# Turning the first-layer output of a fused attention and two-MoE kernel on the vector engine and the DMA queue

## The chip, the cores and the metric

The kernel runs on one core of one Trainium2 chip, in one launch. The metric is device time in microseconds. Three runs of the kernel before took 1084.47, 1084.37 and 1082.22 us, with a median of 1084.37. One execution was profiled: it took 1082.45 us, of which 1080.7 us lie between its first and its last instruction. Engines are named as in the profile: PE is the tensor engine's matmuls, PEld its weight loads, DVE the vector engine, ACT the scalar engine, POOL GpSimd, SP the engine that issues nearly all DMAs.

## The reference

Three layers follow each other, all in float32 except two weight matrices given as float64.

```python
# attention: 8 batches, 8 heads, 576 positions, head size 64, mask in blocks of 64
scores = q @ k.T / 8;  scores[block_i < block_j] = -1e9
attn = softmax(scores);  x = attn @ v                     # x: 4608 tokens x 512
# first dense pair (float64 weights): 512 -> 2048 -> 512
h = x @ w_in;  g = where(h > 0, h, exp(min(h, 0)) - 1);  y = g @ w_out
# soft mixture of 8 experts with 4 slots each
logits = y @ phi                                          # 4608 x 32
d = softmax(logits, over tokens);  slot_in = d.T @ y
slot_out[e] = relu(slot_in[e] @ w1[e]) @ w2[e]
out = softmax(logits, over slots) @ slot_out
```

## The kernel before

The kernel never forms y. It folds `phi` into `w_out` once (WP = w_out @ phi, 2048 x 32), takes the logits of a token straight from g, and gathers d.T @ g (32 slots x 2048) over all tokens; `w_out` is applied to that small result at the end.

The work is cut in four parts.

1. **Start.** 16 chunks each of `w_in` and `w_out` come in as raw float64 words, are narrowed on ACT or POOL and DVE, and become two rounded halves (w_in: `first_weights`) or a float32 copy in DRAM and WP (w_out: `second_weights`). Some space of later tiles serves as staging.
2. **Attention**, in 32 pairs of heads (`pair_load`, `pair_prep`, `pair_scores`, `pair_weights`, `pair_values`). Scores go through exp on ACT to an SBUF buffer PB (two copies, one per pair parity), are scaled on POOL, turned by 128x128 on PE (line 312, att), copied out and multiplied by V (lines 573 and 581). The product enters a ring of x columns, from which token tiles are read.
3. **Token tiles**, 36 of 128 tokens (`moe_tile`, the last two by `last_tiles`). A tile's x is split in two rounded halves (lines 598, 600). For each of four ranges r of 512 hidden units, `tile_range` runs 4 x 3 matmuls (lines 613 to 615) into one of two PSUM banks, ACT takes the exp (618), DVE finishes the nonlinearity (620, 623) into a slot of g. Then four 128x128 transposes on PE (line 312, g) turn the range into one PSUM bank, and ACT or DVE copies it (288 or 290) to gt. `tile_logits` multiplies gt with WP (line 636). After the four ranges `tile_dispatch` takes maxima and exps and adds d.T @ g (line 686) to an accumulator (690). A g slot is free again when line 686 has read it; there are six.
4. **Tail** (`tail`): 36 pieces of 1 MB each (w_out copy, w1, w2 of the experts) are loaded into space that becomes free (lines 749 and 763), the experts run (806, 827, 849), and the output is formed (916).

**What sets the order.** Nothing is left to a scheduler on the chip. `Plan.add` records each step with the engines that may do it, an assumed duration, what it reads and writes, and a key. `Plan.order` plays the steps through on the host, each free engine taking the ready step of the lowest key, and writes each engine's program in that order. So each engine runs a fixed list, and one that meets a wait holds all that stands behind it. SP's list holds the q, k and v loads, and at the end the 1 MB pieces. Where the played PE would be idle in the start or the tail, small bf16 filler matmuls are put in (line 948).

Of the kernel before, what the change touches and what calls it, by code (L numbers as in the profile page):

```python
# [18 lines left out]
P = 128  # L19
# [7 lines left out]
KWS, KWOS, KA0, KAS, KCON, KLD, KSTAGE, NPB = 3.5, 1.0, -109.0, 14.0, -98.0, 30.0, 26.0, 4  # L27
# [170 lines left out]
def attention_moe_kernel(ctx: ExitStack, tc, q, k, v, w_in, w_out, phi, w1, w2, consts, out):  # L198
# [34 lines left out]
    PB = aa.take(2 * PW)  # L233
    PAD = aa.take(12 * PIECE - aa.size)
# [86 lines left out]


    def start():
# [3 lines left out]
        def init(e):  # L327
            nc.vector.memset(f(ACC, 512), 0.0)
            nc.vector.memset(f(SM, 160), 0.0)
            nc.vector.memset(f(sum_col, 20), 1.0)  # L330
            nc.vector.memset(f(NMX, 2), 1e30)
# [3 lines left out]
        def zero(e):  # L335
            for s in range(2):
                nc.gpsimd.memset(f(PB + PW * s + S, 64), 0.0)
            for s in range(NV):
                nc.gpsimd.memset(f(V + 640 * s, 640, 64, P).rearrange("p (h x) -> p h x", h=2)[:, :, 256:320], 0.0)
        add("POOL", 0.9, zero, w=[("p", "b", s) for s in range(2)] + [("v", s, 2) for s in range(NV)], key=k0)  # L340


# [3 lines left out]
               [(GT + 1024 * j, 512, [("gt", 2 * j), ("gt", 2 * j + 1)]) for j in range(2)] + \  # L346
# [112 lines left out]
    def pair_scores(n, fill, key):  # L459
        s = n % 2  # L460
        qt, kt = QT + S * s, KT + S * s
        banks, bkeys = ((H0, H0 + 512), [("h", 0), ("h", 1)]) if n < 4 and fill % 2 else ((SB0, SB0 + 512), [("sb", 0), ("sb", 1)])
        units = FILLS[fill]

        def at(x):
            return banks[0] + 224 if x == "b" else banks[x[1]] + (384 if x[0] == 0 else 0)

        def keys(x):
            return bkeys if x == "b" else [bkeys[x[1]]]

        def sc(e):
            if fill == 0:
                for h, y in ((0, 0), (1, 1), (0, 1), (1, 0)):
                    mm(pb(at("b") + 288 * y, 288, 64 * h, 64 * h + 64), lhsT=f(qt + 512, 64, 64 * h, 64 * h + 64),  # L474
                       rhs=f(kt + 288 * y, 288, 64 * h, 64 * h + 64), start=True, stop=True)
                return
            for u, h in units:
                mm(pb(at((u, h)), P * (u + 1)), lhsT=f(qt + P * u, P, 64 * h, 64 * h + 64),  # L478
                   rhs=f(kt, P * (u + 1), 64 * h, 64 * h + 64), start=True, stop=True)
        cols = S if fill == 0 else sum(wide(x) for x in units) // 2  # L480
        add("PE", 0.2 + cols / 600, sc, r=[("qt", s), ("kt", s)], w=bkeys, key=key)
        for x in units:
            if x != "b":
                add("DVE", 0.11, lambda e, x=x: nc.vector.memset(pb(at(x) + P * x[0] + 64, 64, 0, 64), MASKED), w=keys(x), key=key)
        for x in units:
            c = nm_col + 9 * s + UNITS[x][0]
            add("DVE", 0.08 + wide(x) / 960, lambda e, x=x, c=c: nc.vector.tensor_reduce(  # L487
                out=f(c, 1), in_=pb(at(x), wide(x)), axis=AX.X, op=ALU.max, negate=True),
                r=keys(x), w=[("nm", s, x)], key=key)
            add("ACT", 0.42 + wide(x) / 1300, lambda e, x=x, c=c: nc.scalar.activation(  # L490
                f(PB + PW * s + UNITS[x][1], wide(x)), pb(at(x), wide(x)), AF.Exp, bias=f(c, 1), scale=1.0,
                accum_out=f(sum_col + 9 * s + UNITS[x][0], 1)),
                r=keys(x) + [("nm", s, x)], w=[("p", x, s), ("sum", s, fill // 2)], key=key)

    def pair_weights(n, half, key):
# [9 lines left out]
        for x in units:  # L505
            p = PB + PW * s + UNITS[x][1]
            add("POOL", 0.2 + wide(x) / 1050, lambda e, x=x, p=p: nc.gpsimd.tensor_scalar(  # L507
                out=f(p, wide(x)), in0=f(p, wide(x)), scalar1=f(rs_col + 9 * s + UNITS[x][0], 1), scalar2=0.0,
                op0=ALU.mult, op1=ALU.add), r=[("rs", s, half)], w=[("p", x, s)], key=key)
# [26 lines left out]
        for gi, (blocks, outs) in enumerate(groups):  # L536
            tb, tk = (POST, "post") if gi % 2 and n < NPB else (PTB, "ptb")

            def tr(e, blocks=blocks, tb=tb):
                for j, (x, c) in enumerate(blocks):  # L540
                    transpose(pb(tb + P * j, P), f(PB + PW * s + UNITS[x][1] + P * c, P))
            add("PE", 0.02 + 0.108 * len(blocks), tr, r=[("p", x, s) for x in {b[0]: 0 for b in blocks}] + ["con"], w=[tk], key=key, load=0.0)
# [20 lines left out]
    def pair_values(n, key):  # L563
# [7 lines left out]
        def first(e):  # L571
            for h in range(2):
                mm(pb(PTB, 64, 64 * h, 64 * h + 64), lhsT=f(vs + 320 * h, D), rhs=f(pts[h], 64), start=True, stop=True)
        add("PE", 0.17, first, r=rd, w=["ptb"], key=key, load=0.25)
        add(*evict(n, 64), lambda e: copy(e, f(XR + RING * p + ring, 64), pb(PTB, 64)), r=["ptb"], w=[("xr", p, b % 2, 0)], key=key)
        for c in range(5):
            q0 = max(64, P * c)

            def pv(e, c=c, q0=q0):
# [3 lines left out]
            add("PE", 0.02 + (S - q0) / 603, pv, r=rd, w=["pvb"], key=key, load=0.25)  # L583
# [5 lines left out]
    tslot = [(GT + 512 * j, ("gt", j)) for j in range(4)]  # L589
# [15 lines left out]
    def tile_range(i, r, hb, gs, ts, kr):  # L605
        s = i % 2
        xh, xl = XH + 512 * s, XL + 512 * s
        (g, gk), (gt, tk) = gs, ts
# [17 lines left out]

        def gtr(e):
# [3 lines left out]
        add(CP2, cpdur(512), lambda e: copy(e, f(gt, 512), pb(GTB, 512)), r=["gtb"], w=[tk], key=kr)  # L631

    def tile_logits(r, ts, bank, bk, kp):
# [4 lines left out]
        add("PE", 0.3, lg, r=["wp", ts[1]], w=[bk], key=kp, load=0.25)  # L638
# [55 lines left out]
    def moe_tile(i, key):  # L694
        gs = [gslot[(4 * i + r) % NG] for r in range(4)]
        tile_split(i, key - 6)
        for r in range(4):
            tile_range(i, r, r % 2, gs[r], tslot[r], key + 5.5 * r)
        for r in range(4):
            tile_logits(r, tslot[r], POST, "post", key + 17)  # L700
        tile_dispatch([i], [gs], [(POST, "post")], [(LPS, "lps")], (DTX, "dtx"), (DX, "dx"), key + 17)

    def last_tiles(i, key):

        order = [gslot[(4 * i + j) % NG] for j in range(NG)] + tslot[2:]
# [13 lines left out]
    def tail(key):  # L719
        att = [(nm, s, a) for nm in ("rq", "rk") for s in range(2) for a in range(4)] + [(nm, s) for nm in ("qt", "kt") for s in range(2)] + \  # L720
              [("v", s, j) for s in range(NV) for j in range(3)] + [("p", x, s) for x in UNITS for s in range(2)] + \
# [12 lines left out]
        slots = [(lambda j=j: f(PT + PIECE * j, PIECE).rearrange("p (c d) -> p c d", d=512), att) for j in range(12)]  # L734
        slots += [(ring(hf), xk[hf]) for hf in range(2)]
        slots += [(held("w%d" % r, j), wk[r]) for r in range(4) for j in range(2)]
        slots += [(held("xhl", 0), hk), (lambda: f(GT, PIECE).rearrange("p (c d) -> p c d", d=512), [("gt", r) for r in range(4)])]
# [118 lines left out]
        def late(x, n, dtype, p0=0, p1=P):  # L856
            nm = "w3" if x < 2 * PIECE else "xhl"
# [4 lines left out]
        for m in range(9):  # L862
            handover([("cpkh", m)], sum((pkeys(j) for j in ((20, 21) if m < 8 else (22,))), []))
        handover([("sop", 0), ("sop", 1)], pkeys(22))
# [38 lines left out]
        places = [p1[1, g][1] for g in range(4)] + [23]  # L903
# [79 lines left out]
```

## Time and profile before

| | before |
|---|---|
| median of three runs | 1084.37 us (1082.22 to 1084.47) |
| profiled execution | 1082.45 us, span 1080.7 us |
| PE busy | 1034.6 us, 96% of the span |
| DVE, ACT, POOL busy | 617.5, 499.5, 275.6 us |
| bytes moved by DMA | 97.95 MB, most in the first 150 us and the last 200 us |

A group of the profile reads: line, engine, operation, names written and read, shape, count, then busy us and the mean ns of one, then idle us of the engine just before and who ended most of it. A matmul in float32 stands as two records; a transposing one as one. The duration of a matmul contains its way through the array, so that the distance from one start to the next is what it costs on a full PE. `128*32` ahead of a shape says that the matmul uses a part of the array, 128 rows by 32 columns; four such run beside each other.

### The profile page before, as it was taken

What the parts mean: (1) busy time and instruction counts of PE and PEld (TensorE: products, weight loads), DVE (VectorE), ACT (ScalarE), POOL (GpSimd) and SP (SyncE); (2) the same over time, 40 slices, a digit from 0 to 9 for tenths busy, and PEclk for the clock granted to TensorE, in tenths of its full rate; (3) what the DMA queues carried; (4) which work ended last, traced back from release to release, by engine and by line L of the source; (5) the groups of instructions that cost most, each with busy time, mean ns of one, the idle gap of its engine ahead of it and who ended that gap; (6) DMA issues with size and microseconds to landing.
All of it is one profiled execution on the core that took longest, in us unless ns stands there. A gap on an engine that the chain in (4) does not pass through costs nothing.

```text
span 1080.7 us, 19505 instructions
## 1 busy us (share of the span) xinstructions
PE 1034.6 (96%) x7287; PEld 687.0 (64%) x7287; DVE 617.5 (57%) x1560; ACT 499.5 (46%) x1346; POOL 275.6 (26%) x396
## 2 busy tenths in 40 slices
PE   7878999999999999999999999999999999999993
PEld 4546676666666666666666666666766666767441
DVE  6989663455554555565756665656656564453241
ACT  3766453455454545454544534454444443332134
POOL 4886220122222313122323222231222222010000
PEclk9999889999999999999999999999999999999997
DMA  9988940011111111212111111121110024717969
GB/s 188 201 190 189 229 122 12 18 28 35 33 35 34 34 34 30 38 23 39 29 34 33 35 34 34 23 36 29 30 29 12 1 79 147 282 44 277 348 228 350
DMA packets 219486, 97.95 MB, mean 91 GB/s; under 512 B 192512, under 2 KB 192640, under 8 KB 219392
## 3 DMA queue, kind: packets, MB, share of 16 engines
q1 hardware_dynamic: 217616, 96.49, 34.4%
q8 instruction: 57, 0.93, 0.4%
q10 hardware_dynamic: 1776, 0.22, 0.2%
q14 instruction: 37, 0.30, 0.1%
HBM read 83.05 MB, written 13.63 MB: 89 GB/s over the span
## 4 chain that ended last, share of the span: by engine, by line
PE 86%; DMA 4%; DVE 3%; POOL 2%; SPq 1%; issue 1%; ACT 1%; ACTq 0%; DVEq 0%; POOLq 0%
PE ps L312 16%; PE ps L613 14%; PE ps L615 12%; PE ps L614 12%; PE ps L581 7%; PE ps L478 7%; PE ps L636 4%; PE ps L686 3%; PE ps L474 3%; PE ps L849 1%; POOL att L507 1%; PE ps L827 1%; SPq L307 1%; DMA wo_f<-att 1%; DVE att L374 1%; PE ps L652 1%
## 5 line engine op out<-in xcount | busy, mean ns | idle before, releaser
L613 PE MATMUL ps<-w,xhl 128*128 128x512 f32 x576 | 258.1, 448 | 0.0
L507 POOL TENSOR_SCALAR att<-att,base 128x128 f32<-128x128 f32 (+4 forms) x288 | 173.2, 619 | 246.8 <-DVE base L503 231.2
L615 PE MATMUL ps<-w,xhl 128*128 128x512 f32 x576 | 227.2, 394 | 0.4 <-POOL xhl L600 0.4
L614 PE MATMUL ps<-w,xhl 128*128 128x512 f32 x576 | 226.3, 393 | 0.0
L490 ACT ACTIVATE att<-ps,base 128x128 f32<-128x128 f32 (+4 forms) x288 | 157.4, 553 | 98.9 <-DVE base L487 94.6
L288 ACT COPY att<-ps 128x512 f32<-128x512 f32 (+3 forms) x217 | 106.1, 511 | 123.6 <-PE ps L312 119.0
L312 PE MATMUL ps<-base,att 128*128 128x128 f32 x864 | 140.9, 285 | 11.9 <-POOL att L507 7.4
L620 DVE TENSOR_SCALAR xe<-xe 128x512 f32<-128x512 f32 x144 | 67.6, 469 | 146.4 <-ACT xe L618 145.4
L487 DVE TENSOR_REDUCE base<-ps 128x1 f32<-128x128 f32 (+4 forms) x288 | 137.1, 506 | 23.4 <-PE ps L474 14.7
L312 PEld LDWEIGHTS ps<-base,att 128*128 128x128 f32 x864 | 102.4, 146 | 61.3 <-issue 22.7
L613 PEld LDWEIGHTS ps<-w,xhl 128*128 128x128 f32 x576 | 108.7, 189 | 48.9 <-issue 35.6
L618 ACT ACTIVATE xe<-ps 128x512 f32<-128x512 f32 x144 | 86.1, 598 | 88.5 <-PE ps L615 86.6
L615 PEld LDWEIGHTS ps<-w,xhl 128*128 128x128 f32 x576 | 108.2, 188 | 25.6 <-POOL xhl L600 0.9
L614 PEld LDWEIGHTS ps<-w,xhl 128*128 128x128 f32 x576 | 109.4, 190 | 10.1
L600 POOL TENSOR_TENSOR xhl<-xe,xhl 128x512 fp32r<-128x512 f32 x36 | 47.1, 1310 | 221.4 <-ACT xhl L598 187.7
L478 PE MATMUL ps<-att 64*128 64x128 f32 (+3 forms) x512 | 98.7, 478 | 4.8 <-ACT att L490 4.7
L623 DVE TENSOR_TENSOR g<-xe,ps 128x512 f32<-128x512 f32 x144 | 98.0, 680 | 3.3
L581 PE MATMUL ps<-att 128*64 128x512 f32 (+4 forms) x640 | 94.4, 427 | 0.0
L312 PE MATMUL ps<-base,g 128*128 128x128 f32 x592 | 90.3, 275 | 0.1
L288 ACT COPY g<-ps 128x512 f32<-128x512 f32 (+1 forms) x77 | 44.9, 584 | 87.0 <-PE ps L312 86.0
L312 PEld LDWEIGHTS ps<-base,g 128*128 128x128 f32 x592 | 70.1, 141 | 21.6 <-issue 4.9
L290 DVE COPY g<-ps 128x512 f32<-128x512 f32 (+1 forms) x77 | 52.5, 682 | 42.1 <-PE ps L312 41.5
(115 smaller groups left out, 1089.0 us busy)
## 6 DMA issues: line engine op xcount, KB each, us to landing
att<-in_moe_w_dram SPq DMA_DIRECT2D x12, 1024.0 KB, 13.7
att<-in_k_dram SPq DMA_DIRECT2D x127, 72.0 KB, 2.7
att<-in_q_dram SPq DMA_DIRECT2D x126, 72.0 KB, 2.6
att<-in_v_dram SPq DMA_DIRECT2D x64, 128.0 KB, 2.6
g<-in_moe_w_in_dram SPq DMA_DIRECT2D x16, 512.0 KB, 6.4
w_late<-in_moe_w_dram SPq DMA_DIRECT2D x8, 1024.0 KB, 6.6
att<-in_moe_w_dram SPq DMA_DIRECT2D x32, 256.0 KB, 5.8
out_dram<-att SPq DMA_DIRECT2D x16, 512.0 KB, 5.5
```

The lines of the kernel that those rows point to most:

```text
L288: nc.scalar.copy(o, i)
L312: mm(o, lhsT=i, rhs=f(IDN + base, n, base, base + n), start=True, stop=True, is_transpose=True)
L478: mm(pb(at((u, h)), P * (u + 1)), lhsT=f(qt + P * u, P, 64 * h, 64 * h + 64), rhs=f(kt, P * (u + 1), 64 * h, 64 * h + 64), start=True, sto ...
L487: add("DVE", 0.08 + wide(x) / 960, lambda e, x=x, c=c: nc.vector.tensor_reduce(out=f(c, 1), in_=pb(at(x), wide(x)), axis=AX.X, op=ALU.max, ...
L490: add("ACT", 0.42 + wide(x) / 1300, lambda e, x=x, c=c: nc.scalar.activation(f(PB + PW * s + UNITS[x][1], wide(x)), pb(at(x), wide(x)), AF ...
L507: add("POOL", 0.2 + wide(x) / 1050, lambda e, x=x, p=p: nc.gpsimd.tensor_scalar(out=f(p, wide(x)), in0=f(p, wide(x)), scalar1=f(rs_col + 9 ...
L581: mm(pb(PVB + q0 - 64, S - q0, 64 * h, 64 * h + 64), lhsT=f(vs + 320 * h + D * c, D), rhs=f(pts[h] + CHS * c + q0, S - q0), start=(c == 0) ...
L613: mm(pb(bank, 512), lhsT=fr(xh + P * kk, P), rhs=hi, start=(kk == 0), stop=False)
L614: mm(pb(bank, 512), lhsT=fr(xh + P * kk, P), rhs=lo, start=False, stop=False)
L615: mm(pb(bank, 512), lhsT=fr(xl + P * kk, P), rhs=hi, start=False, stop=(kk == 3))
L618: add("ACT", 0.48, lambda e: nc.scalar.activation(f(ee, 512), pb(bank, 512), AF.Exp), r=[("h", hb)], w=[("e", hb)], key=kr)
L623: add("DVE", 0.6, lambda e: nc.vector.tensor_tensor(out=f(g, 512), in0=f(ee, 512), in1=pb(bank, 512), op=ALU.max), r=[("e", hb), ("h", hb) ...
```

## The change

A tile's g is no longer turned on PE, except for the last two tiles. DVE turns 32x32 blocks within each 32 partitions and writes them, ordered by block, to a new buffer TT (two copies, one per tile parity). When all four ranges of the tile are there, 16 DMAs on SP carry block rows of 32 partitions to block columns of another 32 partitions of gt, 64 KB each. After that one run of 16 matmuls gives the logits.

```diff
-            add("PE", 0.44, gtr, r=[gk, "con"], w=["gtb"], ...)       # tiles 0 to 33
-            add(CP2, cpdur(512), ... copy(e, f(gt, 512), pb(GTB, 512)), r=["gtb"], w=[tk], ...)
+        if ts is None:
+            tt = f(TT + PIECE * s, PIECE).rearrange("p (b c j) -> p c b j", b=4, j=32)[:, 4 * r:4 * r + 4]
+            add("DVE", 0.7, lambda e: nc.vector.transpose(out=tt, in_=f(g, 512).rearrange("p (c b i) -> p c b i", c=4, i=32)),
+                r=[gk], w=[("tt", s, r)], key=kr)
+            return
...
+    def tile_turn(i, kp):
+        s = i % 2
+        for a in range(4):
+            for b in range(4):
+                load(f(GT + 512 * a, 512, 32 * b, 32 * b + 32), f(TT + PIECE * s + 512 * b, 512, 32 * a, 32 * a + 32), 1 << 16,
+                     r=[("tt", s, r) for r in range(4)], w=[("gt", a, b)], key=kp)
+        def lg(e):
+            gt = f(GT, PIECE).rearrange("p (a c j) -> p c a j", a=4, j=32)
+            for c in range(16):
+                j = c % 4
+                mm(pb(POST, P, 32 * j, 32 * j + 32), lhsT=f(WP + NS * c, NS), rhs=gt[:, c], start=(c < 4), stop=(c >= 12))
+        add("PE", 1.0, lg, r=["wp"] + sum((gtk(a) for a in range(4)), []), w=["post"], key=kp, load=0.25)
```

The five steps of a pair's values become one step, so that nothing of another kind stands among their matmuls. Space moves: six g slots become eight, PB has one copy instead of two, the attention area shrinks, and the bank of the g transposes serves half of the late pairs' transposes. The 1 MB pieces of the tail find nine places instead of twelve in the attention area, then the two of TT. The first pairs' keys are set wider apart.

```diff
-KWS, KWOS, KA0, KAS, ... = 3.5, 1.0, -109.0, 14.0, ...
+KWS, KWOS, KA0, KAS, ... = 3.5, 1.0, -116.0, 16.5, ...
-    NG = 6
+    NG = 8
+    TT = ga.take(2 * PIECE)
-    PB = aa.take(2 * PW)
+    PB = aa.take(PW)
-        add("PE", 0.17, first, ...); for c in range(5): add("PE", 0.02 + (S - q0) / 603, pv, ...)
+        add("PE", 2.9, pv, r=rd, w=["ptb", "pvb"], key=key, load=0.25)
-        slots = [(lambda j=j: f(PT + PIECE * j, PIECE)..., att) for j in range(12)]
+        slots = [(flat(PT + PIECE * j), att) for j in range(9)]
+        slots += [(flat(TT + PIECE * j), [("tt", j, r) for r in range(4)]) for j in range(2)]
```

PE in the middle of the program, before: a tile's logits in two runs (line 636), and its g transposes (line 312, g) among the first-layer matmuls and the transposes of attention (line 312, att).

```order
L636 MATMUL ps<-g,base 32x128 x12
L478 MATMUL ps<-att 128x384 x2
L478 MATMUL ps<-att 128x128 x2
L613 MATMUL ps<-w_68,xhl 128x512
L614 MATMUL ps<-w_68,xhl 128x512
L615 MATMUL ps<-w_68,xhl 128x512
L312 MATMUL ps<-base,att 128x128 x4
L312 MATMUL ps<-base,g 128x128 x4
L613 MATMUL ps<-w_68,xhl 128x512
L614 MATMUL ps<-w_68,xhl 128x512
L615 MATMUL ps<-w_68,xhl 128x512
L312 MATMUL ps<-base,att 128x128 x4
L636 MATMUL ps<-g,base 32x128 x4
```

PE in the middle of the changed program (the first-layer lines are 614 to 616 there, the logits line 652).

```order
L614 MATMUL ps<-w_70,xhl 128x512
L615 MATMUL ps<-w_70,xhl 128x512
L616 MATMUL ps<-w_70,xhl 128x512
L652 MATMUL ps<-g,base 32x128 x16
L614 MATMUL ps<-w_70,xhl 128x512
L615 MATMUL ps<-w_70,xhl 128x512
L616 MATMUL ps<-w_70,xhl 128x512
L674 MATMUL ps<-base 128x128
L675 MATMUL ps<-base 128x32
```

The g transposes are gone from the list, and a tile's logits stand in one run, which now waits for the last of the tile's 16 DMAs.

SP at the end of the attention, before: the last v loads, and then the 1 MB pieces, the w_out copy (wo_f) first.

```order
L307 DMA att<-in_v_dram 128x4x64 x2
L307 DMA att<-in_v_dram 64x2x64
L749 DMA att<-wo_f_73 128x4x512 x4
L749 DMA att<-in_moe_w_dram 128x2x1024 x8
L749 DMA xe<-in_moe_w_dram 128x4x512 x2
```

SP at the same place in the changed program. `g<-g` are the turning DMAs, 16 per tile; the names TT and gt lie in the area g.

```order
L308 DMA g<-g 32x512 x48
L773 DMA att<-wo_f_73 128x4x512 x4
L773 DMA att<-in_moe_w_dram 128x2x1024 x5
L773 DMA xe<-in_moe_w_dram 128x4x512
L308 DMA g<-g 32x512 x48
L773 DMA g<-in_moe_w_dram 128x2x1024
L773 DMA xe<-in_moe_w_dram 128x4x512
L308 DMA g<-g 32x512 x10
L773 DMA w_late_8387<-in_moe_w_dram 128x2x1024
L773 DMA w_late_8387<-in_moe_w_dram 128x4x512
L308 DMA g<-g 32x512 x6
```

Ten pieces of 1 MB now stand on SP between the turning DMAs of tile 29 and those of tile 30, and two more within those of tile 33.

## Rows read from the trace of the kernel before

**Rows 1.** The page: busy times of the engines, and shares of the last chain.
```profile
PE 1034.6 (96%) x7287; PEld 687.0 (64%) x7287; DVE 617.5 (57%) x1560; ACT 499.5 (46%) x1346; POOL 275.6 (26%) x396
...
PE 86%; DMA 4%; DVE 3%; POOL 2%; SPq 1%; issue 1%; ACT 1%; ACTq 0%; DVEq 0%; POOLq 0%
```

**Rows 2.** By stage: busy PE, PEld, DVE, ACT, POOL; clock, DMA share, GB/s.
```profile
0.00:91.00 91.00, 70.92 (x576) 46.91 (x576) 76.84 (x165) 53.80 (x144) 66.74 (x83) 0.94 0.94 191
...
150.00:930.00 780.00, 779.94 (x5369) 522.23 (x5368) 440.47 (x1182) 370.44 (x1029) 186.91 (x287) 1.00 0.18 41
...
995.00:1081.00 86.00, 65.40 (x551) 32.08 (x548) 26.50 (x52) 26.42 (x55) 0.00 (x0) 0.90 0.85 306
```

**Rows 3.** Groups by form: busy us, mean ns, idle before and its releasers.
```profile
L623 DVE TENSOR_TENSOR g<-xe,ps 128x512 f32<-128x512 f32 x144 | 98.0, 680 | 3.3
L312 PE MATMUL ps<-base,g 128*128 128x128 f32 x592 | 90.3, 275 | 0.1
L618 ACT ACTIVATE xe<-ps 128x512 f32<-128x512 f32 x144 | 86.1, 598 | 88.5 <-PE ps L615 86.6
...
L620 DVE TENSOR_SCALAR xe<-xe 128x512 f32<-128x512 f32 x144 | 67.6, 469 | 146.4 <-ACT xe L618 145.4
...
L290 DVE COPY g<-ps 128x512 f32<-128x512 f32 x76 | 52.1, 685 | 42.0 <-PE ps L312 41.5
...
L443 DVE STREAM_TRANSPOSE att<-att 128x576 f32<-128x576 f32 x64 | 48.4, 762 | 6.4 <-DMA att<-in_q_dram 4.3 <-DMA att<-in_k_dram 1.2 <-issue 0.8
```

**Rows 4.** PE in order of time: start us, us, line, shape, count.
```profile
403.36 0.60 PE L312 MATMUL ps<-base,g 128*128 128x128 f32 x4
403.72 0.48 PE L613 MATMUL ps<-w,xhl 128*128 128x512 f32 x1
404.03 0.40 PE L614 MATMUL ps<-w,xhl 128*128 128x512 f32 x1
404.27 0.40 PE L615 MATMUL ps<-w,xhl 128*128 128x512 f32 x1
...
410.32 0.40 PE L615 MATMUL ps<-w,xhl 128*128 128x512 f32 x1
410.65 0.64 PE L636 MATMUL ps<-g,base 128*32 128x128 f32 x16
```

**Rows 5.** DMA issue by line (ns, min/median/max), and times to landing at 142:149, 440:446, 42:62.
```profile
L763 SPq DMA_DIRECT2D att<-in_moe_w_dram x32: 327/362/2939, 1006.9 to 1039.5; - x32
...
L307 SPq DMA_DIRECT2D att<-in_q_dram x126: 328/490/2729, 0.7 to 782.9; - x126
...
wo_f<-att SPq DMA_DIRECT2D x3, 256.0 KB, 2.1
...
att<-in_q_dram SPq DMA_DIRECT2D x4, 72.0 KB, 2.5
...
att<-in_q_dram SPq DMA_DIRECT2D x7, 72.0 KB, 7.2
```

**Rows 6.** The 1 MB pieces: SP in order, landing at 906:922, the stage 920:930.
```profile
881.78 25.73 SPq L749 DMA_DIRECT2D att<-wo_f  x4
907.60 11.64 SPq L749 DMA_DIRECT2D att<-in_moe_w_dram  x8
...
att<-in_moe_w_dram SPq DMA_DIRECT2D x8, 1024.0 KB, 17.2
...
920.00:930.00 10.00, 10.00 (x66) 7.00 (x64) 4.88 (x11) 2.96 (x6) 0.37 (x1) 1.00 1.03 408
```

**Rows 7.** PE in a dispatch with nothing beside it, 998:1003.
```profile
998.81 0.49 PE L652 MATMUL ps<-base 128*128 128x128 f32 x2 [0.25 <-DVE base L648]
...
1001.08 0.44 PE L312 MATMUL ps<-base,xe 128*128 128x128 f32 x2 [0.30 <-ACT xe L661]
...
1002.11 1.48 PE L686 MATMUL ps<-g,xe 128*32 128x512 f32 x10 [0.32 <-DVE base L869]
```

**Rows 8.** The stage 140:150, columns as in rows 2.
```profile
140.00:150.00 10.00, 8.30 (x38) 6.94 (x39) 8.46 (x20) 6.45 (x20) 0.59 (x1) 0.65 0.42 150
```

More of the change, by code (lines that the diff above doesn't have):

```diff
@@ L320, in handover, with gtk @@
             plan.readers.setdefault(b, []).extend(sorted(ops))
+    def gtk(a):
+        return [("gt", a, b) for b in range(4)]
     def start():
@@ L411, in give_back @@
             handover(["c"], [("wot", 0), ("wot", 1)])
+            handover([("tt", 0, r) for r in range(4)], [("narrow", 0), ("narrow", 1)])
             handover([("e", 0), ("e", 1)] + [("xr", p, 1, j) for p in range(2) for j in range(2)], [("stage", 5)])
@@ L569, in pair_values, with pv @@
         ring = S * (b % 2)
-        def first(e):
+        def pv(e):
             for h in range(2):
                 mm(pb(PTB, 64, 64 * h, 64 * h + 64), lhsT=f(vs + 320 * h, D), rhs=f(pts[h], 64), start=True, stop=True)
[L574 to L579, printed above, removed]
+            for c in range(5):
+                q0 = max(64, P * c)
                 for h in range(2):
@@ L588, in attention_moe_kernel @@
     gslot = [(G + 512 * j, ("g", j)) for j in range(NG)]
-    tslot = [(GT + 512 * j, ("gt", j)) for j in range(4)]
+    tslot = [(GT + 512 * j, gtk(j)) for j in range(4)]
     def tile_split(i, key):
@@ L637, in lg @@
                    start=(r == 0), stop=(r == 3))
-        add("PE", 0.3, lg, r=["wp", ts[1]], w=[bk], key=kp, load=0.25)
+        add("PE", 0.3, lg, r=["wp"] + ts[1], w=[bk], key=kp, load=0.25)
     def tile_dispatch(tiles, gs, banks, lps, dtx, dx, kp):
@@ L733, in ring, with flat @@
             return lambda: f(XR, 4 * RING).rearrange("p (c t) -> p c t", t=RING)[:, :, S * hf:S * hf + 512]
[L734 to L737, printed above, removed]
+        def flat(o):
+            return lambda: f(o, PIECE).rearrange("p (c d) -> p c d", d=512)
+        wslot = [(held("w%d" % r, j), wk[r]) for r in range(4) for j in range(2)]
+        slots = [(flat(PT + PIECE * j), att) for j in range(9)]
+        slots += [(flat(TT + PIECE * j), [("tt", j, r) for r in range(4)]) for j in range(2)]
+        slots += wslot[:1] + [(ring(hf), xk[hf]) for hf in range(2)] + wslot[1:]
+        slots += [(held("xhl", 0), hk), (flat(GT), sum((gtk(r) for r in range(4)), []))]
         for j, (_, olds) in enumerate(slots):
@@ L862, in tail @@
         for m in range(9):
-            handover([("cpkh", m)], sum((pkeys(j) for j in ((20, 21) if m < 8 else (22,))), []))
-        handover([("sop", 0), ("sop", 1)], pkeys(22))
+            handover([("cpkh", m)], sum((pkeys(j) for j in ((17, 18) if m < 8 else (21,))), []))
+        handover([("sop", 0), ("sop", 1)], pkeys(21))
         for s in range(2):
@@ L902, in tail @@
                 op0=ALU.mult, op1=ALU.add), r=[bk[2 * hf], "con"], w=[("sop", hf)], key=ko)
-        places = [p1[1, g][1] for g in range(4)] + [23]
+        places = [p1[1, g][1] for g in range(4)] + [15]
         NO = len(places)
```

48 lines of the change are left out of this document (23 added, 25 removed).

## The prediction

> **What bounds the kernel now.** I read the page first: PE is busy 96% of the span and carries 86% of the chain that ended last [rows 1]. Is that true of every stage? The table by stage says: from 150 to 930 us PE is busy 779.94 of 780 us at a granted clock of 1.00 (2.4 GHz), while DVE is at 440 (56%), ACT at 370 (47%) and DMA at a share of 0.18. That is the stretch of the token tiles, and there every nanosecond off PE's list is a nanosecond off the time, as long as no new wait comes in. In the first 91 us DMA is at 0.94, and after 995 us at 0.85 with PE at 65 of 86 [rows 2]: there PE's work is not the measure. The groups name what the change takes away: 592 g transposes of 90.3 us in the records, and half of their copies, 76 on DVE at 685 ns [rows 3].
>
> **What goes from PE.** The records overlap, so the price is read from starts. Four g transposes start at 403.36, the next matmul at 403.72: 0.36. That matmul then takes 0.31 to the next start, where the one after it takes 0.24: 0.07 more [rows 4]. A group costs about 0.44 us (with the 0.233 that stands between most first-layer starts). 34 tiles x 4 = 136 groups go; tile 0's four lie in the start, where PE isn't the bound. 132 x 0.44 = 58 us.
>
> A change of the array's shape also costs: from 410.32 a first-layer matmul takes 0.33 to the start of a logits run, 0.10 more than 0.233 [rows 4]. In the order, tiles 1 to 34 have 360 changes of shape into something other than a first-layer matmul before and 246 after, since logits and values now stand in one run each: 114 x 0.10 = 11, and 7 returns fewer to the first layer, 1. Together 12 us. I assume that reading gt in pieces of 32 columns costs the logits nothing; no row shows such a read, and if it doubled their 1 us per tile, that would be +34, if it changed nothing 0. I take 0, since 32 columns of float32 are a whole run of 128 bytes.
>
> So PE's list is 70 us shorter, 2.1 us per tile.
>
> **What comes in on DVE and ACT.** Per tile DVE gets four transposes. The nearest row is 762 ns for 576 columns [rows 3], by columns 0.68 for 512: 2.7 us per tile, less about two copies of 0.685, so +1.4 us in some 22, from 56% to about 63%. It stays far from full, but each step of a chain through it waits longer at times. I put 4 us on that (0 to 10). ACT loses the other half of the copies.
>
> **The new path per tile.** After a tile's last first-layer matmul come exp 0.598, two DVE steps 0.469 and 0.680, and the transpose 0.68 [rows 3], with 0.2 for each of four handoffs (an allowance): 3.2 us. Then SP issues 16 DMAs. A plain 128x512 one holds SP 0.362, a q load with its many short runs 0.490 [rows 5]; with some 0.05 between two, 0.41 to 0.54. I take 0.475, between the two. The last issue comes 15 x 0.475 = 7.1 later, and it lands after 2.1, as 256 KB did on an idle queue (2.5 for a q load in the tile stage) [rows 5]. In all 12.4 us. Against it stands what PE has to do between that matmul and the logits run: added up over the changed order with the prices above, 12.6 to 18.4 us, median 14.1. So on the typical tile 1.7 us is left, which a DVE queue of two or three steps uses up. I put 0.2 us on each of 33 tiles, 7 us. The ends: 0, and with 0.54 per issue and 2.5 to landing (13.8) plus 1.5 of queueing some 1.2 per tile, 40.
>
> The Trainium skill speaks against the 16 transfers. It (the Trainium skill, DMA: Bandwidth & Descriptors, Rules for kernel authors) says to join many small transfers, as below 64 KB one pays mostly overhead, and that transfers to separate groups of partitions run one after another since each is spread over all 16 DMA engines. The Trainium skill's table of sizes (same page, Bandwidth) gives 0.95 us for 64 KB, by which an estimate of 16 in a row is 15 us and the sum would be some 160 us higher. The rows speak against a whole transfer's time for each: q loads of 72 KB are issued 0.54 apart and still land in 2.5 each [rows 5].
>
> **The collision at the end of the attention.** This is where I expect most to be given back. The 1 MB pieces start when the last pair's values are done, since they use the attention's space. Before, nobody in the tiles waits for them. Now tile 30's 16 DMAs stand on SP behind ten of them. In the row of before the third wo_f piece and those behind it are let go near 907 us [rows 6], when the last values end; call that zero. Two pieces are ahead, eight more follow at 1.05 MB / 408 GB/s = 2.6 us each [rows 6]: 21, plus 3 to landing, plus up to 2.7 of the first two, plus 2.6 for tile 30's own megabyte. That is 27 to 30. That small transfers wait behind large ones on this queue the start shows: the same q load lands in 7.2 instead of 2.5 [rows 5]. Meanwhile PE's list has, between the last values and tile 30's logits, 75 first-layer matmuls (17.5), tile 29's logits and dispatch (2.5) and some changes of shape: 20.4. So PE stands 7 to 10 us, 8.5. It can't go on around it: two ranges of tile 32 fill both banks, and their g slots wait for tile 30's dispatch. That dispatch then runs with nothing beside it: in [rows 7] 1.8 us lie between the end of its first step (998.81 + 0.49) and 1001.08, 0.6 before 1002.11, and with the logits' copy ahead and the nonlinearity behind 4 in all. After such a pause the granted clock falls: PE at 8.30 of 10 us had a mean of 0.65 [rows 8]; 3 us at half speed. Sum 16 (0 if the small ones overtake, 25 if all ten are in front and the clock stays low for longer).
>
> **Start and tail.** In the start the order holds 449 fillers (line 948) up to tile 1 where it held 325: the host found PE idle more often when it played the steps through, because the first pairs are set wider apart and PB has one copy. The chunks of w_out, which set the end of the start, come as before. +6 (0 to 12). The tail has DMA as its bound (0.85) [rows 2]; nine pieces instead of twelve fit early, two more when tile 33 is turned, so about one of 2.6 us comes late, and tile 33's DMAs are split around two pieces: +4 (0 to 8).
>
> **Sum.** -58 - 12 + 4 + 7 + 16 + 6 + 4 = -33. From the profiled execution, 1080.7 of span and 1.75 around it, 1082.45: 1049.5, say 1050. The median of three is 1.9 higher, within their own spread; I leave 1050.
>
> **Rivals.**
> *The turned tile is late every time* (slower). The place is the logits run on every tile, the price what 16 issues take over 0.475. Each 0.1 us more per issue makes the path 1.5 longer. With 0.70 it is 15.8, PE waits 1.7 on each of 33 tiles, 56 instead of 7: 1099. The time is above that of before once the wait passes 1.2 per tile, a path of 15.3, or an issue of 0.67. For it: the margin is only 1.7, and landing took 7.2 in the crowded start [rows 5]. Against: in the tile stage DMA has a share of 0.18, and a megabyte per tile more is 2.6 us of its time in 22. 12%.
> *Each transfer waits for the one before it* (a rule of the Trainium skill, above, at work in this kernel). 16 x 2.1 = 34 us per tile against 22: the path would be 37, PE would wait 23 on each tile, 1050 + 33 x 23 = 1800. Against it the q loads above. With the 0.95 of the Trainium skill's table the sum would be near 1210. 2%.
> *The collision is small and the margin holds*: the pieces let the small transfers through, and PE never waits on a tile: 1050 - 16 - 7 + 4 for what a dispatch alone costs = 1031. For it: each DMA engine may have room between pieces. Against: the 7.2 above, and DMA at a share of 1.03 while the pieces run [rows 6]. 13%.
> *More is given back than I see*: the start 12, the collision 25, the tail 8, DVE 10, 2 per cent of PE's list standing: 1050 + 6 + 9 + 4 + 6 + 8 = 1083, no change. For it: the three places follow each other and each is read from few rows. 11%.
> My forecast, 1040 to 1068, has the remaining 62%.
>
> **How the numbers follow.** Runs differ by 0.2%, so less than that is no change. Faster: 62 + 13, and half of the rivals' near ends, 81%. Same: 5%, from the last rival. Slower: 14%, the first two rivals. The range goes from 1030 to 1083: below the collision rival's time hardly anything is left, above it lie the first two rivals.
>
> **What would show it.** No g transposes on PE for tiles 0 to 33, PE's starts 2.1 us per tile closer, and still 100% busy from about 160 to 860 us: right in the main term. Idle PE ahead of the logits line, released by DMA on tiles 5 to 28, would show the late tile; SP's rows then tell whether issue or landing is long. One gap of 8 us or so after the last values, with a lower clock behind it, would show the collision; no gap there, and I was wrong about the queue. Wrong altogether: the tiles as far apart as before.

## The result, and the profile after

Four runs of the changed kernel took 1091.46 to 1094.02 us, median 1092.03, against 1084.41 for the kernel before: a ratio of 1.0078, with a 95% interval of 1.0060 to 1.0097. It is 0.8% slower; I had said 1050. In the profiled executions the span goes from 1080.7 to 1092.2 us, 11.5 us more where the medians differ by 7.6. So some 4 us of what the two profiles show below are scatter between executions.

The page, busy times and the shares of the last chain, to be read beside [rows 1]:

```profile
PE 978.4 (90%) x6888; PEld 658.8 (60%) x6888; DVE 654.5 (60%) x1622; ACT 462.3 (42%) x1288; POOL 268.5 (25%) x391
...
PE 47%; SPq 22%; DMA 14%; DVE 8%; issue 4%; ACT 2%; POOL 1%; ACTq 0%; DVEq 0%; POOLq 0%
```

PE has 56 us less to do, as intended, but carries 47% of the chain instead of 86%. SP, the engine that issues DMAs and had 1%, now has 22%. That is a first sign of where the gain went; the waits below show it.

The stages of [rows 2], and two places near the end (busy PE, PEld, DVE, ACT, POOL; clock, DMA share, GB/s):

```profile
0.00:91.00 91.00, 66.55 (x562) 47.31 (x563) 71.54 (x152) 49.42 (x130) 58.25 (x74) 0.87 0.85 185
150.00:930.00 780.00, 731.64 (x4910) 493.04 (x4912) 488.23 (x1280) 343.19 (x1001) 194.85 (x300) 0.98 0.38 84
995.00:1081.00 86.00, 76.07 (x657) 39.33 (x649) 28.30 (x56) 30.22 (x61) 0.00 (x0) 0.97 0.80 296
...
910.00:940.00 30.00, 9.26 (x60) 5.65 (x59) 5.01 (x13) 1.70 (x7) 0.00 (x0) 0.60 0.59 185
980.00:990.00 10.00, 5.21 (x45) 4.51 (x45) 1.21 (x5) 1.09 (x5) 0.00 (x0) 0.71 1.03 348
```

The middle is no longer full: PE is busy 731.64 of 780 us, and there is one deep hole between 910 and 940. The waits name the cause of both (engine, line, whom it waited for; us in all, times, longest):

```profile
PE ps L652 <- DMA g<-g: 49.5, 27, 17.3
```

Line 652 is the logits run, g<-g the turning DMAs. It is the wait that the change brought in: 27 times, 49.5 us in all, the longest 17.3. Cut at the first first-layer matmul of tiles 2, 30, 33 and 35, the two spans compare like this:

| stretch | before | after | change | I had expected |
|---|---|---|---|---|
| start to tile 2 | 185.3 | 196.5 | +11.2 | +6 |
| tiles 2 to 30 | 706.9 | 679.9 | -27.0 | about -50 |
| tiles 30 to 33 | 53.6 | 71.4 | +17.8 | about +10 |
| tiles 33 to 35 | 33.3 | 28.7 | -4.7 | -4 |
| tile 35 to the end | 101.5 | 115.7 | +14.2 | +4 |

Against what I had expected, the middle is short by 23 us, the tail by 10, tiles 30 to 33 by 8 and the start by 5.

**The middle, one tile.** PE around tile 9's logits (start us, us; the end of a row is the wait ahead of it; a logits matmul has two records):

```profile
406.98 0.40 PE L616 MATMUL ps<-w,xhl 128*128 128x512 f32 x1
407.81 1.08 PE L652 MATMUL ps<-g,base 128*32 128x128 f32 x32 [0.44 <-DMA g<-g]
408.83 0.50 PE L614 MATMUL ps<-w,xhl 128*128 128x512 f32 x1
```

DVE's last turn of that tile, and the issue of its DMAs on SP:

```profile
395.32 0.71 DVE L631 STREAM_TRANSPOSE g<-g 128x512 f32<-128x512 f32 x1
```
```profile
396.21 10.04 SPq L308 DMA_DIRECT2D g<-g  x16
```

The last turn on DVE ends at 396.03, SP issues for 10.04 us, and the logits run starts 11.6 us after the first issue, 0.5 us too late. The durations of these issues (ns, min/median/max), to be set beside [rows 5]:

```profile
L308 SPq DMA_DIRECT2D g<-g x544: 507/589/5373, 167.4 to 978.0; - x182
```

The same DMAs with the median us from issue to landing:

```profile
g<-g SPq DMA_DIRECT2D x544, 64.0 KB, 2.0
```

An issue takes 0.589, and 0.633 lie from one to the next, where I had taken 0.475. The landing is about what I expected.

Over tiles 2 to 29 the trace gives, from the end of a tile's last first-layer matmul to the landing of its last DMA, 15.2 us in the median, where I had 12.4. The work that PE has in that time is about 14.4 us, where I had 14.1.

**The end of the attention.** SP, in order of time:

```profile
890.38 2.63 SPq L773 DMA_DIRECT2D att<-wo_f  x4
893.11 8.07 SPq L773 DMA_DIRECT2D att<-in_moe_w_dram  x5
901.22 2.66 SPq L773 DMA_DIRECT2D xe<-in_moe_w_dram  x1
904.29 27.76 SPq L308 DMA_DIRECT2D g<-g  x17
```

PE in the same stretch:

```profile
929.56 1.94 PE L652 MATMUL ps<-g,base 128*32 128x128 f32 x32 [17.28 <-DMA g<-g]
931.90 0.80 PE L674 MATMUL ps<-base 128*128 128x128 f32 x2 [0.40 <-DVE base L670]
...
935.02 1.94 PE L708 MATMUL ps<-g,base 128*32 128x512 f32 x8 [0.28 <-DVE base L698]
938.42 0.79 PE L614 MATMUL ps<-w,xhl 128*128 128x512 f32 x1 [1.47 <-DVE g L624]
939.01 0.63 PE L615 MATMUL ps<-w,xhl 128*128 128x512 f32 x1
```

Ten pieces, then tile 30's sixteen DMAs (and the first of tile 31's). Only seven of the sixteen are issued before the last piece lands at 922.24. SP's own waits from 900 to 930 say why:

```profile
SPq L308 <- DMA att<-in_moe_w_dram: 5.7, 3, 2.0
SPq L308 <- DMA xe<-in_moe_w_dram: 3.4, 1, 3.4
```

SP's DMAs use eight semaphores in turn, so each of them waits until the DMA eight places ahead of it on SP has landed; in the whole trace none of 1013 starts before that. Four of tile 30's DMAs wait in this way for a piece of 1 MB, 9.1 us in all, and the first of the sixteen takes 5.4 us to issue. The other nine follow the last piece, the last of them lands at 929.26, and PE stands still for 17.28 us. The dispatch then runs alone until 938, and first-layer matmuls take 0.63 instead of 0.40: the granted clock has a mean of 0.60 in 910 to 940, between its two levels.

### The profile page after: what moved, and what is told of

It reads as the page before. It is cut to its first block, busy times and chain, and to the rows that moved or that the text cites. A ratio compares the mean times of both kernels' runs of the same rounds, so it can differ in the third digit from the quotient of the medians.

```text
span 1092.2 us, 19426 instructions
## 1 busy us (share of the span) xinstructions
PE 978.4 (90%) x6888; PEld 658.8 (60%) x6888; DVE 654.5 (60%) x1622; ACT 462.3 (42%) x1288; POOL 268.5 (25%) x391
## 4 chain that ended last, share of the span: by engine, by line
PE 47%; SPq 22%; DMA 14%; DVE 8%; issue 4%; ACT 2%; POOL 1%; ACTq 0%; DVEq 0%; POOLq 0%
SPq L308 21%; PE ps L614 8%; PE ps L313 7%; PE ps L616 6%; PE ps L615 6%; DMA g<-g 5%; PE ps L482 4%; PE ps L652 4%; PE ps L581 4%; PE ps L708 3%; DMA wo_f<-g 2%; DMA xe<-in_moe_w_dram 2%; DMA g<-in_moe_w_in_dram 2%; DVE g L377 1%; PE ps L478 1%
## 5 line engine op out<-in xcount | busy, mean ns | idle before, releaser
L511 POOL TENSOR_SCALAR att<-att,base 128x128 f32<-128x128 f32 (+4 forms) x288 | 168.8, 604 | 264.6 <-DVE base L507 181.7
L494 ACT ACTIVATE att<-ps,base 128x128 f32<-128x128 f32 (+4 forms) x288 | 157.8, 553 | 145.9 <-DVE base L491 134.8
L614 PEld LDWEIGHTS ps<-w,xhl 128*128 128x128 f32 x576 | 110.9, 192 | 64.2 <-issue 35.6
L313 PE MATMUL ps<-base,att 128*128 128x128 f32 x800 | 121.0, 286 | 19.6 <-DMA base<-in_consts_dram 8.5
L616 PEld LDWEIGHTS ps<-w,xhl 128*128 128x128 f32 x576 | 110.2, 191 | 25.7
L313 PEld LDWEIGHTS ps<-base,att 128*128 128x128 f32 x800 | 95.0, 147 | 50.3 <-POOL att L511 20.6
L615 PEld LDWEIGHTS ps<-w,xhl 128*128 128x128 f32 x576 | 111.1, 193 | 14.4
L631 DVE STREAM_TRANSPOSE g<-g 128x512 f32<-128x512 f32 x136 | 94.2, 694 | 4.2 <-PE ps L313 0.9
L581 PE MATMUL ps<-att 128*64 128x512 f32 (+4 forms) x640 | 88.3, 422 | 0.0
L652 PE MATMUL ps<-g,base 128*32 128x128 f32 x1088 | 39.3, 287 | 52.0 <-DMA g<-g 49.5
L449 POOL TENSOR_SCALAR att<-att 128x576 f32<-128x576 f32 x32 | 22.4, 701 | 214.6 <-DVE att L447 153.2
L581 PEld LDWEIGHTS ps<-att 128*64 128x64 f32 x640 | 43.3, 137 | 42.4 <-issue 33.1
```

Of the source, the lines that this page charges most:

```text
L313: mm(o, lhsT=i, rhs=f(IDN + base, n, base, base + n), start=True, stop=True, is_transpose=True)
L581: mm(pb(PVB + q0 - 64, S - q0, 64 * h, 64 * h + 64), lhsT=f(vs + 320 * h + D * c, D), rhs=f(pts[h] + CHS * c + q0, S - q0), start=(c == 0) ...
L614: mm(pb(bank, 512), lhsT=fr(xh + P * kk, P), rhs=hi, start=(kk == 0), stop=False)
L615: mm(pb(bank, 512), lhsT=fr(xh + P * kk, P), rhs=lo, start=False, stop=False)
L616: mm(pb(bank, 512), lhsT=fr(xl + P * kk, P), rhs=hi, start=False, stop=(kk == 3))
```

## The experiments

Each ratio comes from a comparison with the kernel before on the same chip; its medians there were 1084.4 to 1085.9 us. The lists of `Plan` are made on the host; where only an assumed number or a key differs, the chip gets the same work in another order (the number of fillers can differ).

### The assumed issue time

```diff
-        add(engs, tuple(0.48 if x == "SP" else 0.67 for x in engs), ...)
+        add(engs, tuple(ti if x == "SP" else 0.67 for x in engs), ...)      # ti = 0.48, in tile_turn 0.635
```


> One number differs: the host's order assumes 0.635 us for the issue of a turning DMA (measured 0.634 apart) in place of 0.48, so the logits run is put later in PE's list. Theory A (the order was written for a path that is 2.4 us too short): the waits ahead of the logits line in tiles 2 to 29 fall from 23.8 us to under 6, tiles 2 to 30 take 660 to 665 us in place of 680, and the time is 1092 - 18 = 1074 (1066 to 1080). Rival B (the path is longer than what PE has to do in that time, whatever the order): the waits stay above 15 us, perhaps at another line (the g slots), and the time stays within 5 us of 1092. In both, tile 30's wait of 17 us remains.

Measured (`issue_cost`): 1053.64 us, ratio 0.9705 (0.9675 to 0.9736). Tiles 2 to 30 take 645.5 us, and no wait for a turning DMA is left there; the two that remain are tile 30's and tile 33's. The stage, and the waits of the whole span:

```profile
193.00:838.00 645.00, 643.05 (x4423) 429.99 (x4425) 432.77 (x1149) 319.44 (x937) 179.78 (x277) 1.00 0.38 77
```
```profile
PE ps L652 <- DMA g<-g: 18.1, 2, 16.5
```

The DMAs are no faster: 12.05 us in the median from a tile's first issue to its last landing, 11.5 before. So it was not the path that cost the time but the order, written for a path of 9.5: between a tile's last first-layer matmul and its logits run the list now holds 17.6 us of work in the median, instead of some 14.4. The gain is twice what I gave it: beside the 24.6 us of waits some 10 more went from these tiles. Up to 5 of them are the clock (a mean of 0.9925 over these 680 us in the changed kernel, 1.00 here) and some 2 are other waits; the other 3 stay open.

The same number was also moved the wrong way.

```diff
-                     ..., w=[("gt", a, b)], key=kp)
+                     ..., w=[("gt", a, b)], key=kp, ti=0.33)
```

> The changed kernel with the issue of a turning DMA assumed at 0.33 us in place of 0.48; nothing on the chip takes longer or shorter, only the order differs. Theory A (what PE waits is the real path less the assumed one): the assumed path is 16 x 0.15 = 2.4 us shorter, the waits ahead of the logits line in tiles 2 to 29 grow from 23.8 to 60 to 90 us, and the time is 1130 to 1160. Rival B (the wait has to do with how crowded SP or DVE is, and the order matters little): waits of 20 to 35 us, the time 1085 to 1105.

Measured (`assumed_033`, once): 1220.04 us. Its waits, and the stage 200 to 998:

```profile
PE ps L652 <- DMA g<-g: 126.7, 33, 13.0
```
```profile
200.00:998.00 798.00, 698.50 (x4441) 471.34 (x4442) 444.44 (x1185) 310.13 (x911) 177.73 (x279) 0.92 0.30 63
```

A is right in direction and I was short in size. 98 of these 126.7 us lie in 28 waits from 200 to 998 us, 3.5 each where it was 0.9: 2.6 more, about the 2.4 by which the assumed path was shortened. But with a pause of 3.5 us on each tile the granted clock falls to 0.92, which I had not counted, and the matmuls take longer too: tiles 2 to 30 take 118 us more than in the changed kernel, of which the waits are 73.

### The pieces

```diff
-            add("SP", 0.48, fn, r, pkeys(j), kp, 1 << 20)        # piece()
+            add("SP", 1.8, fn, r, pkeys(j), kp, 1 << 20)
-        pw = [piece(..., key - 80, ...)]      p1, p2 with key - 79, -78, -77, -76
+        pw = [piece(..., key - 48, ...)]      p1, p2 with key - 47, -46, -45, -44
```


> Only the place of the 1 MB pieces in SP's list differs: three of them instead of ten stand ahead of tile 30's turning DMAs, and none inside those of tile 33; fewer are under way when the tiles end. Theory A (PE stood still because the turning DMAs queued behind the pieces): the waits of 17.7 us (tile 30) and 5.2 us (tile 33) fall below 3 each, the low clock behind them goes, tiles 30 to 33 take 54 to 58 us in place of 71, and the time is 1092 - 20 = 1072 (1066 to 1078). Rival B (the tail is bound by DMA, so pieces that are held back are missing there): the tail from tile 35 on grows by 2.6 us for each piece late, up to 13, and the time is 1080 to 1090.

Measured (`pieces_yield`): 1074.03 us, ratio 0.9893 (0.9873 to 0.9912). SP in order of time, and PE at tile 30's logits:

```profile
888.07 1.95 SPq L773 DMA_DIRECT2D att<-wo_f  x3
894.60 12.00 SPq L308 DMA_DIRECT2D g<-g  x16
906.64 0.58 SPq L773 DMA_DIRECT2D att<-wo_f  x1
```
```profile
908.53 1.08 PE L652 MATMUL ps<-g,base 128*32 128x128 f32 x32 [2.24 <-DMA g<-g]
```

Theory A. Tiles 30 to 33 take 54.9 us instead of 71.4; the wait is 2.24 instead of 17.28, though tile 31 now waits 3.3, and the clock is 0.88 from 905 to 930. The stretch from tile 33 to the end goes from 144.4 only to 140.4 (134.8 before): part of B is there too. That fewer pieces are ready when the tiles end would explain it; it was not tried on its own.

### Both

The diffs of `issue_cost` and `pieces_yield` together.

> The two edits of issue_cost and pieces_yield in one kernel: the order assumes 0.635 us for a turning DMA's issue, and the 1 MB pieces stand behind the turning DMAs. Theory A (two separate faults of the order): the gains add, 1092 - 38 - 18 = 1036 (1030 to 1042), tiles 2 to 30 in 645 us and tile 30's wait below 5. Rival B (issue_cost already took part of the second gain): 1044 to 1054.

Measured (`both`): 1032.81 us, ratio 0.9515 (0.9481 to 0.9549). The gains add: 38 and 18 less than the changed kernel's 1092 for each edit alone, 59 for both. All waits for turning DMAs:

```profile
PE ps L652 <- DMA g<-g: 5.1, 3, 2.6
```

### One part of the change alone

In the kernel before, only the values and the logits become one step each.

```diff
-        add("PE", 0.17, first, ...); for c in range(5): add("PE", 0.02 + (S - q0) / 603, pv, ...)
+        add("PE", 2.9, pv, r=rd, w=["ptb", "pvb"], key=key, load=0.25)
-        for r in range(4): tile_logits(r, tslot[r], POST, "post", key + 17)
+        add("PE", 1.0, lg, r=["wp"] + [tslot[r][1] for r in range(4)], w=["post"], key=key + 17, load=0.25)
```


> The kernel before, with its transposes on PE, and two of the change's parts alone: the five steps of a pair's values are one step, and a tile's logits are one step. Theory A (each change of the array's shape costs 0.10 us): some 100 changes fewer, 10 us less PE time, the time is 1074 (1070 to 1078). Rival B (the larger steps block what should go between them, and what is saved is lost in waits): 1082 to 1090, with PE idle or waiting where it was full before.

Measured (`runs_alone`): 1069.13 us, ratio 0.9842 (0.9823 to 0.9861). Theory A, and a little more: tiles 2 to 30 take 696.2 us instead of 706.9, with PE as full as before (the stage):

```profile
184.60:880.80 696.20, 695.40 (x4872) 474.96 (x4871) 417.40 (x1112) 338.52 (x960) 176.23 (x270) 1.00 0.17 32
```

In these tiles the array's shape changes 342 times from one matmul to the next, where it was 415. By that count a change costs 0.15 us, where I had 0.10.

### The start

```diff
-KWS, KWOS, KA0, KAS, ... = 3.5, 1.0, -116.0, 16.5, ...
+KWS, KWOS, KA0, KAS, ... = 3.5, 1.0, -109.0, 14.0, ...
```


> The keys of the first pairs go back to those of the kernel before (-109, 14); PB keeps its one copy. Theory A (the wider keys delay the first tiles): tile 2 starts 8 to 11 us earlier, at 185 to 189 in place of 196.5, and the time is 1081 to 1084. Rival B (the one copy of PB holds the first pairs, and the keys were fitted to that): tile 2 starts at 196 or later, and the time is 1090 to 1100.

Measured (`start_back`): 1089.15 us, ratio 1.0039 (1.0017 to 1.0061); tile 2 starts at 191.7. That is 4.8 earlier than with the wide keys and 6.4 later than in the kernel before, in one profile of each: between A and B.

```diff
-    PB = aa.take(2 * PW)
+    PB = aa.take(PW)            # in the kernel before; ("p", x, s) becomes ("p", x)
```


> The kernel before with one copy of PB instead of two, and nothing else of the change. Theory A (the start's 11 us are the one copy and the wider keys, of which the keys are 5 by start_back): tile 2 starts 4 to 8 us later than in the kernel before, and the time is 1088 to 1093 if the rest hides it nowhere. Rival B (the one copy costs nothing; the other 6 us come from the staging space or from SP): tile 2 starts within 2 us of before, and the time is 1081 to 1086.

Measured (`pb_one`): 1091.51 us, ratio 1.0051 (1.0034 to 1.0067); tile 2 starts at 194.8, 9.5 later, and all that follows is as much later. The medians differ by less, 5.6 us on the same chip. Theory A by the time; the 9.5 lies above its range. In these two kernels the exps of pair n+1's block b are put in PB before the last column block of pair n's has been turned, for the first pairs: with 14 between two pairs' keys the step at +14 is recorded ahead of the one at +16. So a part of the weights is another there, and the two times are those of programs that leave out a wait which one copy of PB needs. It also says why the change sets 16.5: one copy of PB needs more than 16 between pairs.

The last of this kind gives the first pairs two copies again, in the space of TT, on top of `both`.

```diff
-KWS, KWOS, KA0, KAS, ... = 3.5, 1.0, -116.0, 16.5, ...
+KWS, KWOS, KA0, KAS, ... = 3.5, 1.0, -109.0, 14.0, ...
+    def copy_of(n):
+        return (TT + 1024, "p2") if n in (1, 3) else (PB, "p")
+            handover([("tt", j, r) for j in range(2) for r in range(4)], [("p2", x) for x in UNITS])
```


> As both, with a second copy of PB for pairs 1 and 3, laid into TT, which no tile uses until these pairs are done, and with the first pairs' keys of the kernel before (-109, 14). Theory A (the start's 11 us come from the one copy and from the wider keys that it needs): tile 2 starts at 185 to 188 in place of 192.3, all later tiles as much earlier, and the time is 1027 (1024 to 1030). Rival B (the late start comes from elsewhere, as SP's list or the staging space): tile 2 starts at 190 or later and the time is 1030 to 1036.

Measured (`two_copies`): 1029.99 us, ratio 0.9488 (0.9463 to 0.9514), the lowest median here. Tile 2 starts at 189.3 in its profile, 3 us earlier than in `both`: by the time in A's range, by the start between A and B, and the intervals of the two kernels' ratios overlap. In the next kernel, whose start has the same steps, it is 184.7, so a single profile does not settle a few us of the start.

```diff
-            add("SP", 1.8, fn, r, pkeys(j), kp, 1 << 20)
+            add("SP", 1.2, fn, r, pkeys(j), kp, 1 << 20)
```


> As two_copies, but the order assumes 1.2 us of SP for a 1 MB piece in place of 1.8, so five pieces instead of four stand ahead of tile 30's turning DMAs and five more ahead of tile 31's. Theory A (each megabyte that is ahead costs the tile 2.6 us once the margin is used up): the waits of tiles 30 and 31 grow by 2 to 8 us, the tail gets shorter by 2 to 5 us, and the time is up to 6 us above two_copies. Rival B (the tail, bound by DMA, is worth more than the waits): 2 to 6 us below two_copies.

Measured (`pace_12`): 1033.34 us, ratio 0.9542 (0.9501 to 0.9583). Tiles 30 to 35 take 93.3 us instead of 81.7, the tail 105.6 instead of 112.0. Both effects are there, and A's is the larger in the profile; the times do not tell the two kernels apart.

### The sixteen DMAs

```diff
-        for a in range(4): for b in range(4): load(gt block (a, b), TT block (b, a), 1 << 16, ...)
+        load(td, f(TT + PIECE * s, PIECE), 1 << 20, r=[("tt", s, r) for r in range(4)], w=[("td", s)], key=kp)
+        for b in range(4): load(f(GT, PIECE, 32 * b, 32 * b + 32)..., td.rearrange("(a p) (b x) -> b p a x", a=4, b=4)[b], 1 << 18, ...)
```


> As both, but a tile is turned with 5 DMAs in place of 16: one of 1 MB stores TT to DRAM, four of 256 KB read it back with the block rows exchanged (the issue is assumed at 0.48 us there). If the number of issues on SP is what the path costs: first issue to last landing falls from 11.5 us to 8 to 9.5 us, and the time is that of both or up to 8 us lower. Rival (two transfers one after the other, and 2 MB more per tile through DMA): the path is as long or longer, the pieces of the tail come later, and the time is 5 to 15 us above both.

Measured (`both_bounce`): 1092.00 us, ratio 1.0057 (1.0034 to 1.0079). Issues by kind and landing, us:

```profile
turn<-g SPq DMA_DIRECT2D x34, 1024.0 KB, 4.2
...
g<-turn SPq DMA_DIRECT2D x136, 256.0 KB, 5.7
```

Five issues, but 4.2 and 5.7 one after the other: 12.5 in the median from the first issue to the last landing. The rival, but the time is 59 us above `both`, where I had given it 5 to 15. And this order again assumed less, about 10.

```diff
-        load(td, ..., w=[("td", s)], key=kp)
+        load(td, ..., w=[("td", s)], key=kp, ti=2.9)
```


> As both_bounce, but the order is told what that way really takes: 2.4 us more before the four reads, so 12.5 us from the first issue to the last landing. Theory A (the 59 us between both and both_bounce were again an assumed path shorter than the real one): the waits ahead of the logits line in tiles 2 to 29 fall below 6 us, and the time is 1035 to 1048. Rival B (the way through DRAM is worse in itself, by traffic or by a path that varies): the waits stay above 15 us, and the time is 1060 to 1090.

Measured (`bounce_told`): 1061.56 us, ratio 0.9781 (0.9750 to 0.9813): half of the loss went, which is A's part. In tiles 2 to 29 the waits fall from 34.7 us to 8.9, in seven places, where `both` has none:

```profile
PE ps L655 <- DMA g<-turn: 8.9, 7, 2.2
```

The other half stayed, as B has it; whether traffic or a varying path makes it was not separated.

Last, what makes an issue long:

```diff
-        for a in range(4): for b in range(4): load(gt block (a, b), TT block (b, a), 1 << 16, ...)
+        for b in range(4):
+            for a in range(2): load(gt block (a, b), TT block (b, a), 1 << 16, ...)
+            ... nc.sync.dma_start(out=f(GT + 1024, 512, 32 * b, 32 * b + 32), in_=w1[b, 32 * (i % 16):32 * (i % 16) + 32, 0:512])
+            ... nc.sync.dma_start(out=f(GT + 1536 + 128 * b, 128), in_=f(TT + PIECE * s + 1536 + 128 * b, 128))
```


> Of a tile's 16 turning DMAs, eight stay (32 partitions by 512, SBUF to SBUF), four read the same shape from w1 in DRAM, and four move 128 partitions by 128 columns from SBUF to SBUF; so half of gt holds other data than it should. Theory A (a DMA within SBUF costs SP more to issue, whatever its shape): 0.55 to 0.62 us for the two kinds within SBUF, 0.33 to 0.40 from DRAM. Rival B (few partitions with long rows cost more): 0.59 for 32 partitions from either side, below 0.45 for 128 partitions. Rival C (the issue is slow because SP issues 16 in a row): the same 0.59 for all three.

Measured (`issue_kinds`, one run, 1070.26 us), the issues in ns, min/median/max: within SBUF 32 by 512, from DRAM 32 by 512, within SBUF 128 by 128.

```profile
L308 SPq DMA_DIRECT2D g<-g x272: 508/590/4490, 169.0 to 953.0; - x136
...
L648 SPq DMA_DIRECT2D g<-in_moe_w_dram x136: 331/578/1651, 170.3 to 953.6; - x136
L651 SPq DMA_DIRECT2D g<-g x136: 510/511/1876, 171.0 to 954.3; - x136
```

A is out: from DRAM it takes as long. Shape gives 0.08 (B, in part). C is out as it stands, since the third kind differs; and in the trace of the changed kernel the first of a tile's sixteen takes 0.537 (median of 23) when SP has issued nothing for over 2 us, so that standing in a row gives some 0.05. None comes near the 0.36 of a 128x512 load of 256 KB [rows 5]. What sets the other 0.10 stays open.

## Why the prediction was wrong

**What goes from PE** was right. `issue_cost` shows tiles 2 to 30 without the waits: 61.4 us less than before. `runs_alone` puts 10.7 of that on the changes of shape, so the 112 groups of transposes are 50.7, 0.45 each (I had 0.44); with the 97 changes of shape fewer that its trace shows, at 0.15, they are 0.42. A logits run takes 1.02 to the next start (407.81 to 408.83), and 1.01 in `runs_alone`, where gt is read plainly: reading it by 32 columns costs nothing, as assumed. DVE's transpose takes 0.694 (0.68), and PE's waits on DVE in tiles 2 to 29 are 2.4 us, inside the 4 that I had put on it.

**The new path per tile** is the step that failed, and the largest miss, 23 us in tiles 2 to 30. "I take 0.475, between the two", I wrote of the issue, with 0.54 as the upper end; it is 0.633. That is 2.4 us per tile, more than the 1.7 of margin, and most of the 2.8 by which the whole path came out longer (15.2 for 12.4). The q loads' 0.490 had been the dearest issue among my rows, and I took it for an upper end though it was only the nearest kind. This is the first rival, to which I gave 12%, and by its own rule (15 x 0.158 over the margin of 1.7) it gives 0.7 per tile; measured are 0.9. What I also missed is that the margin was not a property of the work. The host had played the same 16 issues at 0.48 and had put the logits run just behind their end. With 0.635 in the play it puts it later, and there is enough to do in between (`issue_cost`: 17.6 us). So the question was not whether PE has 14 us of work, but by which number the order was made.

**One after another**, the rule of the Trainium skill (DMA: Bandwidth & Descriptors, Rules for kernel authors) for transfers to two separate halves of the partitions, is not contradicted here. Three windows of tile 9, the first and the last around one turning DMA each, show 0.44 us of moving at a DMA share of 0.64, and nothing in between:

```profile
400.58:401.02 0.44, 0.44 (x10) 0.34 (x6) 0.00 (x0) 0.25 (x3) 0.00 (x0) 1.00 0.64 144
401.03:401.20 0.17, 0.17 (x4) 0.17 (x2) 0.00 (x0) 0.06 (x1) 0.00 (x0) 1.00 0.00 0
401.21:401.65 0.44, 0.44 (x3) 0.35 (x3) 0.00 (x0) 0.44 (x1) 0.00 (x0) 1.00 0.64 144
```

But SP's issues, 0.633 apart, keep them apart already, so no run shows what they would do closer together. What the trace speaks against is the price in my second rival, a whole 2.1 us for each: of the 2.0 from issue to landing only 0.45 are moving, and the rest runs beside the next ones. The Trainium skill's advice, in the same place, to join small transfers is not borne out by the one way tried: joined into five by way of DRAM they took 12.5 us, where the sixteen take 12.2 in `both`.

**The collision** was foreseen in its place and its cause, and its size was short: 17.3 us for tile 30 instead of 8.5. PE's work behind the last values (which end at 891.9) was as I had it, 20.3 us against 20.4. The DMAs took 37.3 instead of 27 to 30. I had two of ten pieces ahead of the last values; the first lands at 896.45, after them, and the tenth 30.3 us behind them. And I had the small DMAs already in the queue by then. Nine of sixteen weren't, since each waits for the landing of the DMA eight places ahead of it, and they took another 7.0 us (922.24 to 929.26).

**The start** cost 11.2 instead of 6 and **the tail** 14.2 instead of 4, in these two profiles. The start is in the main the one copy of PB, 5.6 us by the medians of `pb_one` and 9.5 by its profile; single profiles of one start differ by up to 4.6, so the part of the wider keys is not settled. In the tail, tile 33's DMAs, split around two pieces, hold PE for 4.8 us, but that is not the most of it. From tile 33 to the end it is 134.8 before and 144.4 after, 140.4 in `pieces_yield`, and 144.4 again in `both`, where no wait for turning DMAs is above 2.6. There the DMA share is 1.03 behind the tiles:

```profile
930.00:990.00 60.00, 57.19 (x553) 30.18 (x551) 21.32 (x44) 14.70 (x30) 0.00 (x0) 1.00 1.03 382
```

So what fails in this term is its size: more than the one late piece that I had. How many come late was not counted.

The last line of the working had the right way of going wrong as well: "more is given back than I see". The start, the collision and the tail each gave back more than I had in the sum (DVE did not), and I gave 11% to what came, near enough, together with the first rival. The two don't exclude each other, and I had treated them as if they did.

## What to carry to other kernels

Where a fixed order is made on a host, a new operation must be priced there from a trace: an assumed 0.48 for a real 0.633 cost 38 us, and nothing in the operation itself had to change to get them back. Many small DMAs are paid for by the engine that issues them, and a price taken from another shape is a guess with no upper end. Anything that becomes urgent must not stand behind bulk transfers in one queue, neither in the list nor in flight: here each DMA on SP also waits for the one eight places ahead of it.

## What I had not expected

Pauses cost more than their length: 28 waits of 3.5 us (`assumed_033`, one run) go with a granted clock of 0.92, where it is 1.00 without them (`issue_cost`). Behind ten pieces of 1 MB, SP's issue itself stands still, up to 5.4 us for one DMA (589 ns in the median), so that what stands behind it on SP is held as well. And in the kernel before, a q load that is issued with no other DMA under way takes 0.34 (median of 23), one directly behind another q load 0.50 (median of 91): the price of an issue depends on what has just been issued or is under way, and a row of a profile gives it only for its own surroundings.
